# Three DMA latencies in a planner's model, and a new set of ranks, for a chunk-selecting attention with a SwiGLU block behind it

## The chip, the cores and the metric

The kernel runs on one core of a Trainium2 chip. The metric is the device time of one execution in microseconds (us). Beside it stands a profile of one execution; its span is the time from the first to the last instruction.

## The reference

```python
# q, k, v: (4, 8, 768, 64) float32
ub = sum(maximum(q * k_min, q * k_max))     # bound of each query on each chunk of 32 keys
ub = where(causal, ub, -1e9)
top_chunks = argsort(ub)[..., -6:]          # six chunks per query
scores = q @ k.T / 8, kept where the chunk is chosen and key <= query
attn = softmax(scores) @ v                  # -> x: (3072, 512)
xn = x / rms(x) * rms_g
out = (silu(xn @ w_gate) * (xn @ w_val)) @ w_out    # 512 -> 1536 -> 512
```

The inputs are drawn from a normal distribution; the output is float32.

## The kernel before

The 32 heads are handled as 16 pairs of two heads, four pairs to a batch element (`NP`). For each pair the kernel does the following.

- `prep` loads k and q in natural layout (`kload`, `qload`, two DMAs each on SyncE's queue, SP), turns them on TensorE (`kT`, `qT`, L518), copies them from PSUM (`kE`, `qE`, on ScalarE or VectorE), takes the minima and maxima of each chunk (`kmn`, `kmx`), casts k for the scores (`kC`, on GpSimd) and takes the positive part of q (`relu`). `load_v` loads v on GpSimd's queue (POOL).
- The bounds are matmuls (`ub`) of q and its positive part with the minima and the differences. From pair 6 on, two pairs share them (`duo`, L782). They are copied (`ubE`), turned back (`up`), masked (`ubm`), and the sixth largest is found (`max`). `sel` writes 0 or 1 for each chunk beside the cast q (`qN`) in one of two bounce buffers, tile `qn`.
- From pair 3 on, two DMA transposes on SP (`qX`, function `turned`, L558) carry that buffer to the tile `qs`; earlier pairs are turned on TensorE (`selT`, `selC`).
- `scores` multiplies `ke` with `qs` (`sc`, L869), takes the exponential (`exp`, L886), masks the diagonal (`mask`), multiplies with v (`av`, L905), and divides (`xb`).

When all four pairs of a batch element are done, `norm` scales its rows in two halves and turns them: on TensorE for the first batch element (`tp`), by DMA transposes on SP for the others (`xT`, L993). `ffn` then runs 12 steps of `gate` (L1038), `tanh`, `tg`, `val` (L1059), `hh` for each half, and then `po` (L1081), `poE` and the store `out` (L1096). The weights are loaded and cast on POOL's queue in two parts each: `wg`, `wv`, `wo`. 88 matmuls on zeros (`busy`, L346) stand at the lowest rank and fill places where TensorE has nothing else in the plan.

No engine chooses at run time. The function `Order.run` goes through a model of the five engines with a cost for every step, and at each moment takes the ready step with the lowest rank; the order that comes out is emitted once, and each engine works through its own list in that order. A step's rank is the sum of a value for its kind (`RANK`, one table for the first batch element and one for the others) and a value for its place (`TIMES`: `a` is preparation of a pair, `l` its loads, `s` its scores, `n` the norm and `f` the block of a half, `w` the weights). Some copies name two engines and take the one that is free first in the model. A DMA has a load, which the model divides by a rate to get the time on the DMA engines. The four lines that matter here are these:

```python
if s.load > 250000 and dma > t + 3.0:      # a large load waits while the model's DMA is booked
...
if s.load:
    dma = max(dma, t + occ) + s.load / self.RATE      # RATE = 0.21e6 per us
    s.seen = dma + 1.5
```

Of the kernel before, what the change touches and what calls it, by code (L numbers as in the profile page):

```python
# [24 lines left out]

RANK = (
    dict(
        av=322.54, dif=-188.59, eps=-224.95, exp=140.39, kC=-21.2, kE=-26.98, kT=-342.24,
        kload=-68.72, kmn=-914.82, kmx=-233.95, max=-348.3, qC=-27.39, qE=825.6, qN=415.06,
        qT=187.51, qX=464.44, qload=-68.35, relu=-407.91, root=-15.25, sc=372.15, sel=227.85,  # L30
        selC=494.31, selT=-297.7, sq=-125.45, tp=-51.69, tpE=820.25, ub=-638.32, ubE=-943.52,
        ubm=-791.33, up=-275.69, vload=-812.94, xb=-466.6, xs=4.09,
    ),
    dict(
        av=-259.29, dif=-527.49, eps=-1300.51, exp=-91.52, gate=-103.71, hh=53.82, kC=691.52,
        kE=174.13, kT=62.95, kload=344.34, kmn=400.75, kmx=1189.0, mask=146.21, max=-14.89,
        out=-497.46, po=681.38, poE=-473.84, qE=-203.67, qN=402.53, qT=423.51, qX=-950.23,
        qload=228.48, relu=223.42, root=-1267.38, sc=-170.43, sel=672.51, sq=635.32,
        tanh=850.33, tg=69.89, ub=-68.65, ubE=-332.51, ubm=311.82, up=-188.8, val=-96.16,
        vload=-38.35, xT=292.62, xb=-649.94, xs=-92.37,  # L40
    ),
)

TIMES = {
# [15 lines left out]
}  # L60


# [16 lines left out]
class Order:  # L79
# [18 lines left out]
    def run(self, places):  # L98
# [10 lines left out]
        dma = port = 0.0  # L109
# [8 lines left out]
        out = []  # L118
        while len(out) < len(self.steps):
            if not events:  # L120
                stuck = [x for e in waiting for x in waiting[e] if x.start is None]
                raise RuntimeError("no step can go: " + ", ".join(x.name for x in stuck[:20]))
            t = heapq.heappop(events)
            while events and events[0] <= t + 1e-9:
                heapq.heappop(events)
            for e in free:
                if free[e] > t + 1e-9:
                    continue
                best = None
                for s in waiting[e]:  # L130
                    if s.start is not None or s.ready > t + 1e-9:
                        continue
                    if best is not None and (s.rank, s.n) >= (best.rank, best.n):
                        continue
                    if s.load > 250000 and dma > t + 3.0:
                        heapq.heappush(events, dma - 3.0)
                        continue
                    ok, want = True, {}
                    for b in s.opens:
                        if b.slot is not None:  # L140
                            continue
                        if b.sub and count.get(b.sub, 0) + want.get(b.sub, 0) >= self.limits(b.sub, t):
                            ok = False
                        got = sum(h is None or (h.users == 0 and h.done <= t + 1e-9)
                                  for h in held[b.kind])
                        want[b.kind] = want.get(b.kind, 0) + 1
                        if b.sub:
                            want[b.sub] = want.get(b.sub, 0) + 1
                        if got < want[b.kind]:
                            ok = False  # L150
                    if ok:
                        best = s
                if best is None:
                    continue
                s = best
                s.start, s.eng = t, e
                occ = s.occ[e]
                if e == "PE" and t < self.COLD:
                    occ = 2 * occ

                if e == "DVE" and s.port:
                    occ = max(free["POOL"] - t, 0.0) + occ
                    port = t + occ
                elif e == "POOL":
                    occ = max(port - t, 0.0) + occ
                s.seen = t + occ + self.TAIL[e]
                if s.load:
                    dma = max(dma, t + occ) + s.load / self.RATE
                    s.seen = dma + 1.5
                free[e] = t + occ  # L170
                heapq.heappush(events, free[e])
                heapq.heappush(events, s.seen)
                for b in s.opens:
                    if b.slot is None:

                        b.slot = min((i for i, h in enumerate(held[b.kind])
                                      if h is None or (h.users == 0 and h.done <= t + 1e-9)),
                                     key=lambda i: held[b.kind][i].done if held[b.kind][i] else -1.0)
                        held[b.kind][b.slot] = b
                        if b.sub:  # L180
                            count[b.sub] = count.get(b.sub, 0) + 1
                for b in s.bufs:
                    b.users -= 1
                    b.done = max(b.done, s.seen)
                    if b.users == 0 and b.sub:
                        count[b.sub] -= 1
                for x in s.next:
                    x.left -= 1
                    x.ready = max(x.ready, s.seen)
                    if not x.left:  # L190
                        for y in x.engs:
                            waiting[y].append(x)
                        heapq.heappush(events, x.ready)
                for y in s.engs:
                    waiting[y].remove(s)
                out.append(s)
# [5 lines left out]
def kernel(  # L202
# [51 lines left out]
    def add(name, engs, occ, rank, *a, **kw):  # L254
        return order.add(name, engs, occ, rank if isinstance(rank, dict) else {"": rank}, *a, **kw)
# [75 lines left out]
    def make_ident(e):  # L331
# [7 lines left out]
        out=first[:], in_=ident_f[:, 0:1], func=ACT.Exp), [c_id])  # L339
# [80 lines left out]
    def make_tri(e):  # L420
# [11 lines left out]
        load=140000)  # L432
# [37 lines left out]
    def load_v(c, lr):  # L470
        b, h0 = c.b, c.h0

        def go(e):
            nc.gpsimd.dma_start(  # L474
                out=VX[c.v.slot][:, :, 0:D],
                in_=v[b, h0:h0 + 2].rearrange("h (t p) d -> p (h t) d", p=P))

        c.vload = add("v", "POOL", 1.08, rank(lr, b, "vload"), go, c_vx, opens=[c.v], load=450000)

    def prep(c, i0, nb, at, lr):  # L480

# [74 lines left out]
        def turned(bases, buf, dst, name, deps):  # L556
            def move(e, hl):
                nc.sync.dma_start_transpose(  # L558
                    out=dst[c.set.slot][hl][:].rearrange("d (t p) -> d t p", p=P),
                    in_=bases[buf.slot][:, hl * HW:hl * HW + NT * P])  # L560

            return [add(name, "SP", 1.4, rank(at, b, name, hl, "step"), lambda e, hl=hl: move(e, hl),
                        deps, opens=[c.set], uses=[buf], load=200000) for hl in range(2)]

        reds, casts = [], []
        if side_k:
# [589 lines left out]
```

## Time and profile before

| | |
|---|---|
| median of 3 runs | 320.75 us (318.89 to 322.42) |
| the profiled execution | 319.12 us, span 317.4 us, granted clock 1.00 |
| TensorE (PE) | 97% busy, 2835 matmuls |
| VectorE (DVE), ScalarE (ACT), GpSimd (POOL) | 72%, 62%, 32% busy |
| HBM | 28.57 MB read, 6.29 MB written |

In the profile's lines L12 is line 12 of the kernel, `out<-in` are the tiles written and read with their numbers left out, and `<-` behind a wait names what ended it. PE is the queue of matmuls and PEld that of weight loads; SPq and POOLq are queues on which a DMA is issued. A row of the stretches gives the stretch, its length, then the busy time and number of instructions of PE, PEld, DVE, ACT and POOL, the granted TensorE clock, the DMA engines' share and GB/s. A row of the chain or of the timeline gives the start, the duration and the instructions that were merged. A row of groups ends with the total, the mean duration in ns, and the idle time ahead of it.

### The profile page before, as it was taken

The page shows a single profiled execution, that of the slowest core. Times are in us where ns is not written, and L with a number is a line of the kernel's source. Part 1 is how long each engine was busy: PE and PEld are TensorE (multiplying, and loading weights), DVE is VectorE, ACT ScalarE, POOL GpSimd, SP SyncE. Part 2 cuts the span into 40 slices and gives each one's busy share as a digit, 9 for nine tenths or more (in the row PEclk, how much of TensorE's full clock was granted, in tenths as well). Part 3 has the DMA queues.
Part 4 walks back from the last instruction along what each step waited for, and adds up shares of the span by engine and source line. Part 5 has one row for each costly group of instructions (what it writes and reads, how often), then busy time and mean ns, then how long its engine had stood idle before and what let it go on. Part 6 is the DMA issues. An engine that isn't in the chain of part 4 may idle for free.

```text
span 317.4 us, 7652 instructions
## 1 busy us (share of the span) xinstructions
PE 307.9 (97%) x2835; PEld 197.2 (62%) x2856; DVE 227.8 (72%) x650; ACT 197.2 (62%) x429; POOL 102.0 (32%) x157
## 2 busy tenths in 40 slices
PE   8999999999979999999999999999999999999994
PEld 4676778675667656766677555665675565555552
DVE  7799967898779895698995887569657773364410
ACT  5888999784667878863698735863595333233311
POOL 8675532651447544341247401510132000000000
PEclk9999999999999999999999999999999999999999
DMA  9999999999999996992913465200501600101022
GB/s 175 218 188 142 168 170 155 172 154 166 169 154 175 104 132 152 219 207 47 148 31 25 37 174 101 53 33 2 118 16 46 152 5 35 66 0 68 35 98 99
DMA packets 113125, 34.97 MB, mean 110 GB/s; under 512 B 106176, under 2 KB 110016, under 8 KB 113088
## 3 DMA queue, kind: packets, MB, share of 16 engines
q1 hardware_dynamic: 82976, 26.23, 42.9%
q0 software_dynamic: 28512, 7.87, 25.9%
q10 hardware_dynamic: 1600, 0.39, 0.6%
q8 instruction: 22, 0.36, 0.5%
q14 instruction: 15, 0.12, 0.1%
HBM read 28.57 MB, written 6.29 MB: 110 GB/s over the span
## 4 chain that ended last, share of the span: by engine, by line
PE 83%; DMA 6%; ACT 5%; POOL 2%; issue 1%; DVE 1%; ACTq 0%; POOLq 0%
PE po L1081 19%; PE vp L1059 18%; PE gp L1038 18%; PE sc L869 9%; PE av L905 6%; DMA qs<-qn 3%; DMA vx<-in_v_dram 3%; ACT pt L886 3%; PE busy L346 3%; PE ub L782 2%; PE pk L518 2%; PE pq L518 2%; ACT ke L297 1%; POOL ke L301 1%; PE up L804 1%
## 5 line engine op out<-in xcount | busy, mean ns | idle before, releaser
L886 ACT ACTIVATE pt<-sc 128x512 bf16<-128x512 f32 (+3 forms) x192 | 89.3, 580 | 8.4 <-PE sc L869 7.8
L1045 ACT ACTIVATE sg<-gp 128x384 bf16<-128x384 f32 x96 | 47.8, 506 | 55.4 <-PE gp L1038 54.3
L1059 PE MATMUL vp<-xT,wv 128*128 128x384 bf16 x384 | 77.2, 326 | 0.0
L1038 PE MATMUL gp<-xT,wg 128*128 128x384 bf16 x384 | 77.1, 326 | 0.0
L1051 DVE SCALAR_TENSOR_TENSOR tg<-sg,gp 128x384 bf16<-128x384 bf16 x96 | 51.4, 547 | 28.9 <-ACT sg L1045 27.9
L1081 PE MATMUL po<-wo,hh 128*128 128x512 bf16 (+1 forms) x284 | 65.9, 370 | 1.0 <-issue 0.2
L1067 DVE TENSOR_TENSOR hh<-vp,tg 128x384 bf16<-128x384 f32 x96 | 50.9, 549 | 15.2 <-PE po L1081 7.1
L869 PE MATMUL sc<-qs,ke 128*128 128x128 bf16 (+5 forms) x417 | 52.4, 250 | 1.7 <-DMA qs<-qn 1.4
L1038 PEld LDWEIGHTS <-wg 128*128 128x128 bf16 x384 | 35.9, 98 | 24.0 <-issue 1.2
L1059 PEld LDWEIGHTS <-wv 128*128 128x128 bf16 x384 | 36.2, 98 | 22.8
L1081 PEld LDWEIGHTS <-hh 128*128 128x128 bf16 x300 | 29.0, 98 | 28.8 <-issue 1.2
L892 POOL TENSOR_SCALAR_AFFINE_SELECT pt<-pt 128x512 bf16<-128x512 bf16 (+1 forms) x48 | 24.7, 530 | 47.2 <-ACT pt L886 46.9
L905 PEld LDWEIGHTS <-pt 128*128 128x128 bf16 x672 | 32.0, 98 | 10.8 <-POOL pt L892 1.3
L905 PE MATMUL av<-vx,pt 128*128 128x65 bf16 x672 | 37.1, 193 | 1.1 <-DMA vx<-in_v_dram 0.7
L869 PEld LDWEIGHTS <-ke 128*128 128x128 bf16 (+1 forms) x420 | 30.0, 97 | 10.6 <-DMA qs<-qn 1.5
L301 POOL CAST ke<-kt 64x768 bf16<-64x768 f32 x31 | 25.5, 821 | 22.2 <-ACT kt L297 10.6
L299 ACT ACTIVATE osb<-po 128x512 f32<-128x512 f32 (+1 forms) x20 | 11.7, 586 | 30.7 <-PE po L1081 30.6
L346 PE MATMUL busy<-zeros 128*128 128x512 bf16 (+1 forms) x86 | 20.2, 349 | 1.4 <-DVE zeros L341 1.3
L301 POOL CAST qn<-qnat 128x768 bf16<-128x768 f32 x11 | 9.4, 857 | 34.4 <-DMA qs<-qn 34.3
L474 POOL DMA_DIRECT2D vx<-in_v_dram x16 | 16.8, 1049 | 9.3 <-PE av L905 9.0
L982 DVE SCALAR_TENSOR_TENSOR xs<-xb,ri,gains 128x512 bf16<-128x512 bf16 x24 | 17.8, 767 | 1.9 <-DMA xT<-xs 1.6
L926 DVE TENSOR_TENSOR xb<-av,rden 128x384 bf16<-128x384 f32 (+1 forms) x34 | 18.1, 534 | 1.2
(87 smaller groups left out, 306.8 us busy)
## 6 DMA issues: line engine op xcount, KB each, us to landing
out_dram<-osb SPq DMA_DIRECT2D x23, 256.0 KB, 2.1
knat<-in_k_dram SPq DMA_DIRECT2D x30, 192.0 KB, 5.2
qnat<-in_q_dram SPq DMA_DIRECT2D x30, 192.0 KB, 4.9
vx<-in_v_dram POOLq DMA_DIRECT2D x16, 192.0 KB, 6.2
wg<-in_moe_w_gate_dram POOLq DMA_DIRECT2D x2, 768.0 KB, 7.9
wv<-in_moe_w_val_dram POOLq DMA_DIRECT2D x2, 768.0 KB, 7.2
wo<-in_moe_w_out_dram POOLq DMA_DIRECT2D x2, 768.0 KB, 11.9
qs<-qn SPq DMA_TRANSPOSE x26, 2.8
```

Source lines behind the costliest of these rows:

```text
L301: engine[e].tensor_copy(out_, in_)
L346: nc.tensor.matmul(t[:, 0:n], zeros[:, 0:P], zeros[:, 0:n], start=True, stop=True)
L869: nc.tensor.matmul(t[:, x:x + m, :].rearrange("p a b -> p (a b)"), ke[kk, kb * P:(kb + 1) * P], qs[kk, q0 * P:(q0 + m) * P], start=not tri ...
L886: nc.scalar.activation(out=t[:, 0:nn, :], in_=sc.tile[:, 0:nn, :], func=ACT.Exp, scale=SCALE)
L892: nc.gpsimd.affine_select(out=pt.tile[:, 0:nd, :], in_=pt.tile[:, 0:nd, :], compare_op=ALU.is_ge, fill=0.0, base=0, pattern=[[0, nd], [1, ...
L905: nc.tensor.matmul(av.tile[:, qi - i0, :], pt.tile[:, x, :], VX[c.v.slot][:, hl * NT + kb, :], start=(begin and m == 0), stop=(left[0] == ...
L1038: nc.tensor.matmul(t[:], wg[:, g, hs], XT[b].tile[:, g, cols], start=(g == 0), stop=(g == NP - 1))
L1045: nc.scalar.activation(out=t[:], in_=gp.tile[:], func=ACT.Tanh, scale=0.5)
L1051: nc.vector.scalar_tensor_tensor(out=t[:], in0=sg.tile[:], scalar=1.0, in1=gp.tile[:], op0=ALU.add, op1=ALU.mult)
L1059: nc.tensor.matmul(t[:], wv[:, g, hs], XT[b].tile[:, g, cols], start=(g == 0), stop=(g == NP - 1))
L1067: nc.vector.tensor_tensor(out=t[:], in0=vp.tile[:], in1=tg.tile[:], op=ALU.mult)
L1081: nc.tensor.matmul(po.tile[:], hhs[ht].tile[:, th * P:(th + 1) * P], wo[:, ht, c0:c0 + cn], start=(ht == 0), stop=(ht == NHT - 1))
```

## The change

Three numbers of the model change, and both tables of ranks are replaced by others. The steps, their instructions and the functions that emit them stay as they are; which engine makes a copy and where each instruction stands come out of the model again.

```diff
 RANK = (
     dict(
-        av=322.54, dif=-188.59, eps=-224.95, exp=140.39, kC=-21.2, kE=-26.98, kT=-342.24,
...
+        av=490.79, dif=-125.43, eps=-501.19, exp=121.82, kC=-14.0, kE=71.19, kT=-475.34,
...
 TIMES = {
-    "a0": -581.96, "a1": -582.93, "a10": -566.56, "a11": -515.49, "a12": 78.05, "a13": -90.35,
...
+    "a0": 347.98, "a1": 339.24, "a10": 285.13, "a11": 419.78, "a12": 80.87, "a13": 244.6, "a14":
...
                 if s.load:
                     dma = max(dma, t + occ) + s.load / self.RATE
-                    s.seen = dma + 1.5
+                    s.seen = dma + 2.5
...
-        c.vload = add("v", "POOL", 1.08, rank(lr, b, "vload"), go, c_vx, opens=[c.v], load=450000)
+        c.vload = add("v", "POOL", 1.08, rank(lr, b, "vload"), go, c_vx, opens=[c.v], load=600000)
...
             return [add(name, "SP", 1.4, rank(at, b, name, hl, "step"), lambda e, hl=hl: move(e, hl),
-                        deps, opens=[c.set], uses=[buf], load=200000) for hl in range(2)]
+                        deps, opens=[c.set], uses=[buf], load=240000) for hl in range(2)]
```

All entries of `RANK` and `TIMES` have new values; the first line of each stands for them. What this does to the written order, as far as the prediction speaks of it: the first scores stand behind 21.9 us of TensorE work (17.8 before), the scores of pair 5 come after those of pairs 6 and 7, `po` of the first batch element's first half moves from the end of the program to the middle, and the last tile on TensorE is a half `po` tile of the last half.

More of the change, by code (lines that the diff above doesn't have):

```diff
@@ L27 @@
     dict(
-        av=322.54, dif=-188.59, eps=-224.95, exp=140.39, kC=-21.2, kE=-26.98, kT=-342.24,
[L29 to L32, printed above, removed]
+        av=490.79, dif=-125.43, eps=-501.19, exp=121.82, kC=-14.0, kE=71.19, kT=-475.34,
+        kload=87.97, kmn=-874.66, kmx=-133.18, max=-255.93, qC=33.7, qE=845.44, qN=259.26,
+        qT=103.97, qX=345.57, qload=155.84, relu=-499.55, root=257.08, sc=507.34, sel=-26.2,
+        selC=347.24, selT=-149.89, sq=-107.03, tp=-229.09, tpE=761.97, ub=-520.06, ubE=-1040.27,
+        ubm=-713.28, up=-436.98, vload=-613.02, xb=-206.71, xs=77.27,
     ),
     dict(
[L35 to L40, printed above, removed]
+        av=-429.52, dif=-56.01, eps=-1189.67, exp=-151.99, gate=-135.63, hh=1.46, kC=597.83,
+        kE=85.85, kT=171.47, kload=161.93, kmn=616.71, kmx=1102.65, mask=10.34, max=190.89,
+        out=-472.13, po=508.04, poE=-157.3, qE=116.75, qN=127.45, qT=237.68, qX=-949.48,
+        qload=148.26, relu=407.95, root=-1351.08, sc=-302.51, sel=596.25, sq=201.44,
+        tanh=975.67, tg=83.53, ub=-292.03, ubE=-462.41, ubm=235.61, up=30.05, val=-121.8,
+        vload=-3.79, xT=450.72, xb=-572.52, xs=-267.85,
     ),
```

28 rows, old and new, of the table TIMES are left out of this document.

## The prediction

> **What bounds the kernel now.** I read the busy shares first, then PE (TensorE) in five stretches of the span, then the chain that ended last and the waits of PE's two queues, and last the DMAs that these waits name.
>
> ```profile
> span 317.4 us, 7652 instructions
> PE 307.9 (97%) x2835; PEld 197.2 (62%) x2856; DVE 227.8 (72%) x650; ACT 197.2 (62%) x429; POOL 102.0 (32%) x157
> DMA  9999999999999996992913465200501600101022
> PE 83%; DMA 6%; ACT 5%; POOL 2%; issue 1%; DVE 1%; ACTq 0%; POOLq 0%
> ```
> ```profile
> 0.00:32.00 32.00, 29.84 (x306) 19.52 (x308) 27.91 (x92) 24.71 (x50) 23.14 (x42) 1.00 1.28 179
> 32.00:80.00 48.00, 47.62 (x595) 35.00 (x594) 39.93 (x139) 39.02 (x89) 20.42 (x29) 1.00 1.25 166
> 80.00:96.00 16.00, 14.06 (x151) 9.69 (x150) 11.72 (x27) 10.69 (x25) 6.86 (x11) 1.00 1.10 155
> 96.00:312.00 216.00, 214.94 (x1783) 132.34 (x1799) 148.26 (x395) 121.81 (x267) 51.58 (x77) 1.00 0.48 85
> 312.00:317.40 5.40, 1.43 (x9) 0.65 (x7) 0.00 (x0) 0.98 (x2) 0.00 (x0) 1.00 0.20 73
> ```
> The first two columns after the stretch are its length and PE's busy time. PE is busy 307.9 of 317.4 us at a granted clock of 1.00, so 9.5 us are idle: 2.16 before 32 us, 0.38 up to 80, 1.94 between 80 and 96, 1.06 up to 312, and 3.97 in the tail after the last matmul. PE bounds this kernel, and the change gives PE exactly the same instructions in another order. What it can win therefore lies inside those 9.5 us, less a start and a tail that every order has. What it can lose has no such limit. The DMA row says where: the 16 engines are busy at 9 tenths or more for the first 15 slices, about 119 us, and only there does a transfer have to wait for others.
>
> ```profile
> PE sc L869 <- DMA qs<-qn: 1.4, 1, 1.4
> PE busy L346 <- DVE zeros L341: 1.3, 1, 1.3
> PE av L905 <- DMA vx<-in_v_dram: 0.7, 1, 0.7
> 80.82 10.40 DMA qs<-qn
> 72.11 7.87 SPq L498 DMA_DIRECT2D knat<-in_k_dram  x2
> 80.82 6.10 SPq L558 DMA_TRANSPOSE qs<-qn  x2
> 92.08 0.46 DVE L666 SCALAR_TENSOR_TENSOR qn<-m,ubm 128x288 bf16<-128x288 f32 x1 [2.12 <-DMA qs<-qn]
> qs<-qn SPq DMA_TRANSPOSE x26, 2.8
> ```
> The first three rows are all that PE's matmul queue ever waited for that is over 0.3 us. The largest is one event: SP took 7.87 us to issue one k load, the transposes of pair 6 could be issued only behind it, and their landing took 10.40 us where the median is 2.8. PE's wait at the scores was 1.4 us, and VectorE (DVE) stood 2.12 us before it could write the next selection into the same buffer.
>
> **The change part by part.** Only constants change: three latencies in the planner that writes the order, and the ranks it sorts by. I count in "PE work": the rows of PE's own order added up, in which a gate or val group is 0.65 us, four po matmuls 0.86 and the bound of two pairs 1.45.
>
> ```profile
> 72.30 0.65 PE vp L1059 x4
> 72.95 1.45 PE ub L782 x32
> 115.04 5.18 PE po L1081 x24
> ```
> *The longer landings.* A transpose was counted as landing 200000/210000+1.5=2.45 us after its turn on the DMA, and is now counted as 240000/210000+2.5=3.64; a k or q load goes from 3.5 to 4.5, a v load from 3.64 to 5.36.
>
> ```profile
> knat<-in_k_dram SPq DMA_DIRECT2D x30, 192.0 KB, 5.2
> qnat<-in_q_dram SPq DMA_DIRECT2D x30, 192.0 KB, 4.9
> vx<-in_v_dram POOLq DMA_DIRECT2D x16, 192.0 KB, 6.2
> ```
> For the loads (5.2, 4.9 and 6.2 us) the new figures are nearer. For transposes 2.8 lies between old and new. The Trainium skill, DMA: Bandwidth & Descriptors, section "Anatomy of one DMA", gives 2.0 us plus bytes/436e3; for 196608 bytes that is an estimate of 2.45 us, which is the old figure and speaks against counting transposes longer. The trace's 2.8 and 10.40 say that the old figure was too short while the DMA engines are full, so the measurement decides. By the page alone the transposes' part would bring nothing, and the sum below would be 1.0 us higher.
>
> A longer estimate costs no time itself; it spreads the order. After the first loads, a transpose of selections had at least 3.5 us of PE work between issue and first use in the old order and has 4.6 in the new one; k loads at least 5.1 and now 6.5; v loads 6.1 and now 6.9.
>
> *Pair 6.* Old order: q8 and k9 loads stand directly ahead of its transposes on SP. New order: only k9, with 6.2 us of PE work between, and the next load (q11) behind them. Between issue and first use there are 8.8 us of PE work, not 7.9. The wait at 80 to 96 us costs PE 1.94; ends 0 and -1.9. The buffer rotation is as before (pairs 6 and 7 share one bounce buffer) and a 768 KB part of wo starts in the same stretch, so I take half: **-1.0**.
>
> *The weights.* Their place moves the other way. Second half of wg: 19.1 us of PE work between issue and first gate, now 10.3. Second half of wv: 15.9, now 10.2. The last part of wo: 24.8, now 10.5. They go out on GpSimd's (POOL's) queue, behind casts and masks.
>
> ```profile
> wg<-in_moe_w_gate_dram POOLq DMA_DIRECT2D x2, 768.0 KB, 7.9
> DMA to landing us min/median/max: 6.9/7.9/8.9
> DMA to landing us min/median/max: 6.9/7.2/7.5
> DMA to landing us min/median/max: 9.0/11.9/14.8
> ```
> These rows are wg's, then the tiles wg, wv and wo. Against wg's own worst, 8.9, a cover of 10.3 is enough; against wo's worst, 14.8, it is 4.5 short. For the last part of wo the rows are 9.0 (enough) and 14.8 (4.3 short). wg and wv have landed in 6.9 to 8.9 even among loads, and the second wo part that took 9.0 is the one issued in a like place, so I take **0** for both; the ends are +4.5 and +4.3. What hides them is gates, vals and scores of pairs 6 and 7. If wg's part is late, 6 gates and 7 vals queued one behind another on PE wait, and behind them the scores of pair 6; wv's part then has that wait as cover and adds nothing.
>
> *The start.* First loads gain about 1 us of cover, and v of pair 1 moves ahead of q of pair 2. DVE's work up to the selection of pair 2, added in its order, exceeds PE's ahead of the transposes that read it by 3.2 us, and by 2.6 before: **+0.6**. v of pair 0 keeps 6.9 us of cover (7.1 to 7.8 for the first v loads before), so its 0.7 us wait stays: **0**, ends -0.7 and +0.7.
>
> *Who copies.* DVE takes over 3 kt, 5 qt, 5 rt, and one each of ubd, xT and qn, and gives up 4 qs, one dif and two osb.
>
> ```profile
> L301 DVE COPY qt<-pq 128x384 f32<-128x384 f32 x7 | 3.8, 547 | 1.6 <-PE pq L518 1.1 <-PE av L905 0.6
> L636 DVE TENSOR_SCALAR rt<-qt 128x768 f32<-128x768 f32 x3 | 1.7, 557 | 0.3 <-ACT qt L297 0.3
> L301 DVE COPY qs<-st 64x768 bf16<-64x768 bf16 x6 | 3.3, 555 | 0.2
> 152.00:160.00 8.00, 8.00 (x58) 5.50 (x56) 8.00 (x18) 5.20 (x11) 1.48 (x2) 1.00 1.16 164
> 160.00:168.00 8.00, 8.00 (x105) 5.72 (x103) 7.89 (x15) 7.54 (x18) 4.80 (x10) 1.00 0.01 3
> ```
> At some 0.55 us each the sum is +5.2 us on DVE and about as much off ScalarE. DVE is 72% busy, so PE's matmuls hide this: **0**, ends 0 and +5.2, since DVE does have full stretches (8.00 and 7.89 of 8).
>
> *The later stages.* Norm to gate has 14.7 us of PE work at the last batch (12.9 before). The shortest way from the bounds' transposes to the scores is pair 12's, 10.1 us (11.1 before). On it stand four ubm (0.3 each), the maxima (about 2.6), one tg, the selection (0.8) and a landing of 2.8, about 8 us: **0**. The 1.06 us of small gaps stays too; lower end -1.1.
>
> *The end.* Before, the last piece on PE is a full po tile: ScalarE copies it in 0.60 us and its store lands in 2.1. Now it is a half tile.
>
> ```profile
> 312.65 0.38 ACT L299 ACTIVATE osb<-po 128x256 f32<-128x256 f32 x1 [2.88 <-PE po L1081]
> 313.51 0.60 ACT L299 ACTIVATE osb<-po 128x512 f32<-128x512 f32 x1 [0.48 <-PE po L1081]
> out_dram<-osb SPq DMA_DIRECT2D x23, 256.0 KB, 2.1
> out_dram<-osb SPq DMA_DIRECT2D x2, 128.0 KB, 1.8
> ```
> 0.22+0.3: **-0.5**.
>
> Sum: -1.0+0.6-0.5=-0.9 against the profiled execution's 319.12 us (its span of 317.4 and 1.7 around it), 318.2. That execution lies 1.63 below the median of 320.75; on the median's footing I forecast **319.9 us**, no change that can be told.
>
> **The rivals.**
> *A, slower: a weight part lands late.* Place: the first gate on the second half of wg, and the first po. It decides from a landing of 10.3 us, and 10.5 for wo. If the slowest part's 14.8 holds at one place, +4.4 and 324.3; at both, +8.8 and 328.7. For it: full DMA engines, and in the new order five k and q loads stand in the 10 us ahead of wg's part. Against: 6.9 to 8.9 in the same company. By the page named above, 1.57 MB read would take an estimated 5.6 us and A could not occur; the trace's 9.0 to 14.8 disagree.
> *B, slower: DVE becomes the bound.* If all its 5.2 us fall where DVE is full, 319.9+5.2=325.1. For it: the two full windows. Against: added up in order, DVE's work leads PE's by no more by 105 us of PE work than before.
> *C, faster: every wait goes.* -1.9 at pair 6, -0.7 at v, -1.1 of small gaps, -0.5 at the end, nothing at the start: -4.2 and 316.5. For it: covers that are longer nearly everywhere. Against: it must all come together, and every order makes waits of its own.
> *D, the change does nothing:* PE's work is the same and undisturbed transposes land in 2.8 whatever is assumed; 320.3 with the shorter end.
>
> **How the numbers follow.** About 1% (3.2 us) is what a measurement of this kernel tells from no change. The forecast has 0.36, with a range of its own of 318 to 323, and D 0.09: within 1% together 0.45. C has 0.17, because a gain of over 3.2 needs three quarters of all that can be won. A has 0.19 and B 0.19: slower 0.38. The range reaches from C's time, 316.5, to 328.0, just short of both places of A; some 0.05 lie below and 0.12 above.
>
> **What would show it.** PE busy stays near 308 us at clock 1.00. The wait of the scores on qs shrinks below 1.4 us and DVE's 2.12 us goes; if not, that step is wrong. wg's second part lands within 10 us, and no gate or po waits on a DMA; a PE wait on wg, wv or wo of 2 us or more is A. DVE near 233 us with PE waiting on DVE in the middle would be B. The tail is 3.5 us, not 3.97. A PE idle time of over 13 us makes the forecast wrong, wherever it stands.

## The result and the profile after

The changed kernel takes 318.70 us (median of 20 runs, 318.08 to 319.69) and the kernel before, on the same chip, 321.82 us (20 runs, 318.27 to 326.56). The ratio is 0.9934, 95% interval 0.9912 to 0.9955: 0.66% faster, inside the 1% that was called no change. The ratio is taken over the runs within 1.5% of the fastest of their kernel, which leaves out the slowest of the kernel before, and so it lies nearer to 1 than the 0.990 of the medians. The profiled execution takes 318.09 us against 319.12 before, so only 1.0 of the 3.1 us between the medians can be seen between the two profiles; the rest is that the changed kernel's runs lie within 1.6 us of each other and those of the kernel before within 8.3.

The page of the changed kernel, then its stretches (columns as for the kernel before):

```profile
span 316.4 us, 7669 instructions
PE 310.2 (98%) x2856; PEld 197.4 (62%) x2856; DVE 235.6 (74%) x659; ACT 194.5 (61%) x420; POOL 102.1 (32%) x157
DMA  9999999999969999999940036540040046000202
PE 91%; ACT 4%; DVE 4%; issue 0%; ACTq 0%; DVEq 0%
```
```profile
0.00:32.00 32.00, 29.99 (x284) 18.02 (x285) 26.41 (x96) 23.14 (x45) 19.77 (x38) 1.00 1.20 179
32.00:80.00 48.00, 47.31 (x598) 35.17 (x595) 42.75 (x122) 38.55 (x87) 24.01 (x32) 1.00 1.02 165
80.00:96.00 16.00, 16.00 (x133) 10.41 (x132) 12.93 (x33) 8.46 (x19) 4.37 (x7) 1.00 1.20 128
96.00:312.00 216.00, 216.00 (x1845) 133.27 (x1842) 153.52 (x412) 123.62 (x270) 53.91 (x82) 1.00 0.50 87
312.00:316.40 4.40, 0.87 (x8) 0.53 (x6) 0.00 (x0) 0.77 (x2) 0.00 (x0) 1.00 0.30 103
```
TensorE (PE) is idle for 2.01, 0.69, 0, 0 and 3.53 us. The idle stretch between 80 and 96 us (1.94 before) is gone, and DMA is no longer in the chain (6% before). The 1.06 us of small gaps up to 312 us are gone too, but they were hardly idle time: 2856 of 2856 matmuls are recorded here and 2835 before, and nearly all of these gaps (about 0.05 us each) stand within a few rows of a place where a record is missing. For the same reason PE's busy time seems to rise from 307.9 to 310.2.

PE's waits in the changed kernel, all of them over 0.1 us:

```profile
PE busy L346 <- DVE zeros L341: 1.3, 1, 1.3
PE st L695 <- DVE selq L680: 0.7, 1, 0.7
PE gp L1038 <- ACT xT L297: 0.3, 1, 0.3
PE av L905 <- ACT pt L886: 0.2, 1, 0.2
```
None of them is on a DMA. Next the issues on SP's queue around pair 6's transposes, and the landings (minimum, median, maximum) of the tiles wg, wv, wo and qs:

```profile
81.41 2.59 SPq L558 DMA_TRANSPOSE qs<-qn  x2
84.09 1.62 SPq L498 DMA_DIRECT2D qnat<-in_q_dram  x2
```
```profile
DMA to landing us min/median/max: 6.8/7.7/8.6
DMA to landing us min/median/max: 6.8/7.8/8.8
DMA to landing us min/median/max: 7.4/7.6/7.7
DMA to landing us min/median/max: 2.5/2.9/5.5
```
The longest landing of a transpose is 5.5 us where it was 10.40, and wo's parts land in 7.4 to 7.7 where they took 9.0 to 14.8. The DMA row is as full as before (9 tenths or more in 19 of the first 20 slices), so it is not that the engines have room.

The chain's rows that tell where the order stands, and the tail:

```profile
71.89 1.45 PE ub L782 x32
109.01 1.08 PE ub L782 x17
```
```profile
311.83 1.04 PE L1081 MATMUL po<-wo,hh 128*128 128x256 bf16 x8
312.52 0.82 ACT L299 ACTIVATE osb<-po 128x256 f32<-128x256 f32 x2 [1.59 <-PE po L1081]
```
I compare the start of a row with the PE work that the order has ahead of it (counted as in the prediction). Before: 72.95 us with 66.2 ahead, 115.04 with 105.4, so PE runs 6.75 and then 9.6 us late. After: 71.89 with 63.3, 109.01 with 100.2, so 8.6 and then 8.8 late. The start became 1.85 us worse; the stretch from 72 to 110 us became 2.65 better; from there to the last matmul some 0.25 worse; the tail 0.44 better. Together -1.0, which is what the spans show. Little of the loss at the start is idle time (2.01+0.69 us up to 80 us, 2.16+0.38 before); the rest is spread over PE rows that take longer than counted.

### The profile page after: what moved, and what is told of

Read it like the earlier page. It is cut to its first block, busy times and chain, and to the rows that moved or that the text cites. A ratio compares the mean times of both kernels' runs of the same rounds, so it can differ in the third digit from the quotient of the medians.

```text
span 316.4 us, 7669 instructions
## 1 busy us (share of the span) xinstructions
PE 310.2 (98%) x2856; PEld 197.4 (62%) x2856; DVE 235.6 (74%) x659; ACT 194.5 (61%) x420; POOL 102.1 (32%) x157
## 3 DMA queue, kind: packets, MB, share of 16 engines
q0 software_dynamic: 28512, 7.87, 26.0%
## 4 chain that ended last, share of the span: by engine, by line
PE 91%; ACT 4%; DVE 4%; issue 0%; ACTq 0%; DVEq 0%
PE gp L1038 20%; PE vp L1059 20%; PE po L1081 20%; PE sc L869 12%; PE av L905 7%; PE pk L518 3%; PE pq L518 3%; PE busy L346 2%; PE ub L782 2%; PE up L804 1%; ACT ke L297 1%; PE ub L724 1%; DVE ku L549 1%; DVE kmx L547 1%; ACT pt L886 1%; PE sc L875 1%
## 5 line engine op out<-in xcount | busy, mean ns | idle before, releaser
L886 ACT ACTIVATE pt<-sc 128x512 bf16<-128x512 f32 (+2 forms) x192 | 88.9, 594 | 10.3 <-PE sc L869 9.6
L1051 DVE SCALAR_TENSOR_TENSOR tg<-sg,gp 128x384 bf16<-128x384 bf16 x96 | 52.3, 550 | 33.1 <-ACT sg L1045 31.4
L1038 PE MATMUL gp<-xT,wg 128*128 128x384 bf16 x384 | 74.9, 326 | 0.3 <-ACT xT L297 0.3
L1059 PE MATMUL vp<-xT,wv 128*128 128x384 bf16 x384 | 74.8, 326 | 0.0
L1067 DVE TENSOR_TENSOR hh<-vp,tg 128x384 bf16<-128x384 f32 x96 | 51.9, 553 | 10.5 <-PE vp L1059 8.3
L869 PE MATMUL sc<-qs,ke 89*128 89x128 bf16 (+4 forms) x420 | 53.6, 251 | 0.0
L869 PEld LDWEIGHTS <-ke 89*128 89x128 bf16 (+1 forms) x420 | 29.4, 97 | 7.3 <-issue 1.0
L299 ACT ACTIVATE osb<-po 128x512 f32<-128x512 f32 (+1 forms) x22 | 12.8, 582 | 30.8 <-PE po L1081 29.4
L346 PE MATMUL busy<-zeros 128*128 128x512 bf16 (+1 forms) x88 | 19.2, 349 | 1.3 <-DVE zeros L341 1.3
L549 DVE TENSOR_REDUCE ku<-kt 128x24 f32<-128x768 f32 (+1 forms) x17 | 15.2, 897 | 2.7 <-ACT kt L297 2.6
```

What stands on the lines that cost most here:

```text
L346: nc.tensor.matmul(t[:, 0:n], zeros[:, 0:P], zeros[:, 0:n], start=True, stop=True)
L869: nc.tensor.matmul(t[:, x:x + m, :].rearrange("p a b -> p (a b)"), ke[kk, kb * P:(kb + 1) * P], qs[kk, q0 * P:(q0 + m) * P], start=not tri ...
L886: nc.scalar.activation(out=t[:, 0:nn, :], in_=sc.tile[:, 0:nn, :], func=ACT.Exp, scale=SCALE)
L1038: nc.tensor.matmul(t[:], wg[:, g, hs], XT[b].tile[:, g, cols], start=(g == 0), stop=(g == NP - 1))
L1051: nc.vector.scalar_tensor_tensor(out=t[:], in0=sg.tile[:], scalar=1.0, in1=gp.tile[:], op0=ALU.add, op1=ALU.mult)
L1059: nc.tensor.matmul(t[:], wv[:, g, hs], XT[b].tile[:, g, cols], start=(g == 0), stop=(g == NP - 1))
```

## The experiments

Two theories stood at first for pair 6: SP's loads ahead of the transposes made them late, as the prediction had it, or it was the 768 KB weight part that is in flight beside them. The experiments move single steps of the finished order; `done` is the list that `Order.run` returns, and `spot` finds the n-th step of a name at a place.

**e3: before, the first wo part later.**

```diff
     done = order.run(PLACE)
+    s = done.pop(spot("wo", "w3"))
+    done.insert(spot("qX", "a6", 1) + 1, s)
```


> The kernel before, with one weight DMA (the first wo part) issued behind the transposes of pair 6 instead of ahead of them, some 10 us of PE work later; it still has 27 us of PE work before its first use. Theory (the gain of the change is mainly the late transposes of pair 6, and these were late because the DMA engines were full): they land in under 6 us instead of 10.4, PE's idle time between 80 and 96 us falls from 1.94 to under 0.5, the profile comes to about 317, and the runs scatter less than before's 318 to 326. Rival 1 (they were late because SP itself stood 7.87 us at the k load ahead of them): that issue stays above 5 us and PE's wait stays above 1.2. Rival 2 (the gain sits in the tail and the start): no change of the median, about 321.5.

Measured: 323.96 us (12 runs, one of them an outlier of 1142.53), ratio 1.0053 (1.0010 to 1.0096). From SP's timeline, the chain, PE's waits, wo's landings and the stretches after the wait:

```profile
74.05 1.42 SPq L498 DMA_DIRECT2D knat<-in_k_dram  x2
81.82 2.54 SPq L558 DMA_TRANSPOSE qs<-qn  x2
```
```profile
83.08 11.58 DMA qs<-qn
```
```profile
PE av L905 <- POOL pt L892: 3.9, 1, 3.9
```
```profile
DMA to landing us min/median/max: 10.1/11.7/13.3
```
```profile
96.00:98.00 2.00, 1.45 (x22) 1.46 (x23) 1.97 (x6) 0.49 (x2) 0.86 (x2) 0.65 0.78 162
98.00:100.00 2.00, 1.78 (x16) 1.27 (x15) 1.14 (x4) 1.69 (x4) 1.31 (x3) 0.50 0.57 125
```
Neither side had it. The k load ahead, which had held SP for 7.87 us, is issued in 1.42, and SP is free at 75.47 us. Still the transposes go out no earlier (81.82 us, 80.82 in the kernel before), and the second of them takes 11.58 us to land (the first 3.58): now both wo parts, issued at 82.43 and 83.65, are in flight beside it. So SP's slow load was not the cause. The wait is longer than before because GpSimd (POOL) stands at its cast into `qn` until the transposes have landed, and the masks of the exponentials are queued behind it. And the wait costs twice: the granted clock falls to 0.50 behind it.

**e4: after, two loads ahead of pair 6's transposes.** The q and k loads of pair 11 go in front of them.

```diff
+    for name in ("qload", "kload"):
+        s = done.pop(spot(name, "l11"))
+        done.insert(spot("qX", "a6"), s)
```


> The changed kernel, with the q and k loads of pair 11 issued directly ahead of pair 6's transposes on SP instead of behind them. Theory: the transposes are issued and land later, more than 6 us instead of at most 5.5, PE waits 1 to 3 us for them at the scores of pair 6 where it did not wait at all, the median rises from 318.7 to 320 or 321.5, and the runs scatter over more than 2 us. Rival (loads ahead of the transposes do not matter as long as the weights are not in flight): 318.7, PE waits under 0.3 us.

Measured: 318.94 us, ratio 0.9908 (0.9876 to 0.9940). The longest landing of a transpose is 7.0 us (5.5 in the changed kernel) and PE waits for no DMA. But the loads stand ahead in the list only: SP issues them at 66.35 and 71.70 us and is free at 74.89, 7 us before the transposes go out at 81.94. So loads that are issued in good time do no harm that shows; a load that holds SP until the transposes are due was not tried here, and what speaks against that cause is e3.

**e8: before, the second wo part later**, clear of pair 6.

```diff
+    s = done.pop(spot("wo", "w2"))
+    done.insert(spot("v", "l9") + 1, s)
```


> The kernel before, with one weight DMA (the second wo part issued) moved from just behind the issue of pair 6's transposes to behind the v load of pair 9, some 16 us later; nothing else differs. Theory (a weight part in flight beside a pair's transposes makes these land 10 us late and more, which holds up the scores, GpSimd's next cast and the masks behind it): the transposes of pair 6 land in under 6 us, PE's idle time between 80 and 96 us falls below 0.6, the granted clock is 0.998 or more in most runs, and the median falls from 322.0 to 318.5 to 320. Rival 1 (the gain of the change came from its other order as a whole): the median stays above 321. Rival 2 (the wait only moves to the transposes of pairs 8 and 9 or to the first po, which the part now meets): PE idles 1.5 us or more after 105 us.

Measured: 321.36 us (316.67 to 323.92), ratio 0.9952 (0.9897 to 1.0006), which leaves it open whether this gains; 318.5 to 320 was expected. Its two fastest runs, 316.67 and 317.13, lie below every run of the changed kernel. The profiled execution, 322.19 us, is one of its longer ones. Pair 6's transposes now land in 4.7 us on the mean, but those of pair 5 met the second wv part and the first wo part. From the chain, PE's waits and wo's landings:

```profile
68.38 15.43 DMA qs<-qn
```
```profile
PE sc L869 <- DMA qs<-qn: 3.0, 2, 2.5
```
```profile
DMA to landing us min/median/max: 11.3/13.7/16.0
```
Where the weight part went out of the way the landing is short. The longest landing of all runs is not the work of the edit: up to the moved part, at about 81 us, this run has the order of the kernel before, and there the same two transposes of pair 5, beside the same two parts, landed in 7.6 and 10.3 us where they took 13.6 and 15.4 here. One order can thus land up to 6 us later in one execution than in another.

**e11: before, both wo parts clear** of pairs 5 and 6.

```diff
+    s = done.pop(spot("wo", "w2"))
+    done.insert(spot("v", "l9") + 1, s)
+    s = done.pop(spot("wo", "w3"))
+    done.insert(spot("kC", "a9", 1) + 1, s)
```


> The kernel before with both wo parts moved: the first to behind the casts of pair 9 (about 88 us, after pair 6's transposes have landed), the second to behind the v load of pair 9 (about 98 us). The transposes of pairs 5 and 6 then meet no wo part. Theory (weight parts in flight beside the transposes were what the kernel before lost, in its time and in its scatter): both land in 8 us or less, PE idles under 1 us between 56 and 112 us, the granted clock is 0.997 or more in most runs, and the median is 317 to 319.5, below before's 321.7 and perhaps below the changed kernel's 318.7. Rival (the parts only find other victims, pair 7's transposes or the first po): PE waits 1.5 us or more at these places, and the median stays above 320.5.

Measured: 325.62 us, ratio 1.0109 (1.0072 to 1.0146). The stretches, SP's timeline and PE's waits:

```profile
56.00:80.00 24.00, 23.90 (x259) 15.85 (x258) 21.28 (x78) 16.60 (x38) 10.19 (x16) 1.00 1.13 152
80.00:96.00 16.00, 16.00 (x184) 11.59 (x183) 13.49 (x31) 12.19 (x28) 8.70 (x13) 1.00 0.91 119
96.00:112.00 16.00, 8.43 (x71) 5.25 (x77) 5.69 (x11) 6.29 (x13) 5.36 (x8) 0.69 1.25 165
```
```profile
93.22 14.27 SPq L498 DMA_DIRECT2D qnat<-in_q_dram  x6
```
```profile
PE pq L518 <- issue: 7.6, 1, 7.6
```
PE is busy 39.90 of the 40 us from 56 to 96 (37.96 in the kernel before): the cause is confirmed in the old order. But the total came out much as the rival had it: the moved part met three q loads at 93 us, SP needed 14.27 us to issue them, and PE waited 7.6 us at the turning of q (the trace calls it issue), with a granted clock of 0.69 in that stretch. A weight part has to pass somewhere, and the new order has it pass where it meets nothing that is needed soon.

**e9: after, the second wo part put in the way** of pair 6's transposes.

```diff
+    s = done.pop(spot("wo", "w2"))
+    done.insert(spot("v", "l5") + 1, s)
```


> The changed kernel, with its second wo part issued ahead of the landing of pair 6's transposes (behind the v load of pair 5, some 19 us earlier) instead of after pair 7's. Theory: the transposes of pair 6 land in 9 us or more instead of at most 5.5, GpSimd's cast for pair 7 waits as long, PE waits 1 us or more at the scores or at the products behind the masks, the granted clock falls below 0.997 in some runs, and the median rises from 318.7 to 320 or 323. Rival (the longer covers of the new order absorb it): under 319.3, and PE waits under 0.5 us.

Measured: 319.78 us, ratio 0.9956 (0.9926 to 0.9986). The landings of qs and the stretch:

```profile
DMA to landing us min/median/max: 2.5/3.0/9.0
```
```profile
80.00:96.00 16.00, 15.34 (x123) 9.66 (x122) 12.90 (x34) 7.83 (x17) 3.22 (x5) 1.00 1.27 166
```
The slow landing comes back (9.0 us, before 10.40) and with it 0.66 us of idle time, a third of what the old order lost there. VectorE stands 1.1 us before it can write the next selection, and PE 0.5 at a gate that waits for VectorE's product `hh` behind it. Direction and place are as expected, the price is smaller than the 1 us or more that was expected; by the intervals of the times alone it could not be told from the changed kernel.

**e5 and e10: after, the second wv part late**, to try rival A's mechanism: once behind `dif` of pair 8, once behind the first wo part.

```diff
+    s = done.pop(spot("wv", "w1"))
+    done.insert(spot("dif", "a8") + 1, s)     # e5
+    done.insert(spot("wo", "w3") + 1, s)      # e10
```


> The changed kernel, with the second part of wv issued some 5 us later on GpSimd's queue (behind the differences of pair 8). Theory (a weight part lands 6.8 to 8.8 us after its issue, and PE has no slack behind it): PE waits 2 to 4 us at the first val that uses it, and the total rises by as much, to 320.7 to 322.7. Rival (PE's wait is made up later, because ScalarE and VectorE set the pace there): the wait shows but the median stays within 0.5 us of 318.7.

> The changed kernel, with the second part of wv issued behind the first-issued wo part, so that PE waits longer for it than the 1.80 us that it waited when the part was issued behind the differences of pair 8. Theory (a long enough wait of PE costs twice: the wait itself, and about 4 us at a granted clock of 0.5 behind it): PE waits 3 to 7 us in one piece, the granted clock falls to 0.5 for some 4 us after it, and the median rises by the wait and 1 to 2 us more, to 323 to 328. Rival (the clock falls only where several short waits follow each other, as in the run with fewer fillers): the clock stays at 0.998 or more, and the median rises by the wait alone.

Measured: e5 320.28 us, ratio 0.9950 (0.9923 to 0.9978); e10 327.94 us, ratio 1.0215 (1.0169 to 1.0262). PE's waits of e5, then of e10, then the stretches of e10 around its wait:

```profile
PE vp L1059 <- DMA wv<-in_moe_w_val_dram: 1.8, 1, 1.8
```
```profile
PE vp L1059 <- DMA wv<-in_moe_w_val_dram: 6.5, 1, 6.5
```
```profile
84.00:86.00 2.00, 0.00 (x0) 0.00 (x0) 0.00 (x0) 0.00 (x0) 0.00 (x0) 1.00 1.15 176
86.00:88.00 2.00, 0.04 (x1) 0.04 (x2) 0.00 (x0) 0.00 (x0) 0.00 (x0) 0.70 1.39 154
88.00:90.00 2.00, 2.00 (x7) 0.99 (x8) 0.54 (x2) 0.00 (x0) 0.00 (x0) 0.50 1.67 151
90.00:92.00 2.00, 2.00 (x8) 0.92 (x7) 1.04 (x3) 0.00 (x0) 0.24 (x1) 0.50 1.63 160
92.00:94.00 2.00, 2.00 (x9) 0.96 (x8) 1.58 (x3) 0.00 (x0) 0.59 (x1) 0.59 1.44 170
```
In e5 1.8 us of wait cost 1.6 us at a clock of 1.00, somewhat less than the 2 to 4 that were expected. In e10 6.5 us of wait cost 9.2: the clock stays at half for some 6.8 us behind the beginning of the dip (0.70, 0.50, 0.50, 0.59 in four stretches of 2 us). Rival A's mechanism is real and would have been expensive; it did not occur because the weight parts of the changed kernel land in 8.8 us at most.

**e6: after, with the copies on the engines of before.** The steps kE, qE, relu, ubE, tpE, poE and selC keep the new order, and each goes to the engine that it has in the kernel before (some 5 us, net, from VectorE back to ScalarE).

```diff
     done = order.run(PLACE)
+    for e, ns in (("ACT", [...]), ("DVE", [...])):
+        for n in ns:
+            order.steps[n].eng = e
```


> The changed kernel in its order, but each PSUM copy (kt, qt, rt, ubs, ubd, xT, qs, osb) on the engine that the kernel before used for it: some 5 us of work go back from VectorE to ScalarE. Theory (VectorE's extra work is hidden): within 0.7 us of 318.7, either way. Rival (VectorE's load costs time in the changed kernel): 0.7 us or more below, 318.0 or less.

Measured: 324.49 us, ratio 1.0111 (1.0069 to 1.0154), 5.8 us over the changed kernel. The stretch from 32 to 48 us and the first gate, of the changed kernel and then of e6, and a wait of e6:

```profile
32.00:48.00 16.00, 15.90 (x258) 12.92 (x255) 12.35 (x41) 15.50 (x37) 8.82 (x11) 1.00 1.06 139
```
```profile
61.00 0.81 PE L1038 MATMUL gp<-xT,wg 128*128 128x384 bf16 x4 [0.32 <-ACT xT L297]
```
```profile
32.00:48.00 16.00, 15.14 (x232) 11.68 (x232) 8.69 (x34) 15.88 (x38) 8.43 (x10) 1.00 1.03 138
```
```profile
64.86 0.81 PE L1038 MATMUL gp<-xT,wg 128*128 128x384 bf16 x4
```
```profile
PE av L905 <- ACT pt L886: 2.6, 7, 0.6
```
Neither side had it. With the old engines ScalarE is busy 15.88 of 16 us, PE waits 2.6 us for its exponentials where it waited 0.2, and the first gate comes 3.9 us later. The copies are not hidden in this order: on which engine they stand is part of it.

**e13 and e14: after, 1.4 us more off ScalarE.** Two qt and one ubs copy between 34 and 47 us go to VectorE; in e14 12 of the 19 matmuls on zeros at 52 us (1.3 us) are left out as well.

```diff
+    for n in (412, 473, 541):
+        order.steps[n].eng = "DVE"
...
     for s in done:
+        if 306 <= s.n <= 317:      # e14 only
+            continue
```


> The changed kernel with three copies between 34 and 47 us (two qt, one ubs, together 1.4 us of ScalarE) moved to VectorE, TensorE's order untouched. Theory: ScalarE bounds the stretch from 28 to 50 us (15.50 us busy of 16 between 32 and 48), but TensorE has matmuls on zeros there that fill what it would wait, so moving copies alone brings at most 0.5 us: 318.3 to 318.9, and TensorE's idle time between 32 and 80 us falls below 0.69. Rival: VectorE (12.35 of 16 there) is the tighter one, and its norm of the first batch element comes later: over 319.5.

> The same three copies on VectorE, and 12 of the 88 matmuls on zeros (1.3 us) left out of the run of 19 that stands at 52 us. Theory: ScalarE's 1.4 us are what those 12 covered, so TensorE gains about 1 us: 317.4 to 318.2, clock 1.00. Rival: what stands behind the matmuls on zeros is VectorE's norm and not ScalarE's exponentials, so the same wait for the norm opens (over 0.8 us) and the time is 318.5 to 320.

Measured: e13 318.91 us, ratio 0.9951 (0.9916 to 0.9985); e14 318.70 us, ratio 0.9914 (0.9882 to 0.9945): no gain over 318.70. PE's waits of e14:

```profile
PE tp L1004 <- DVE xs L982: 0.7, 2, 0.5
PE busy L346 <- DVE xb L926: 0.7, 1, 0.7
```
The 1.3 us that were left out come back as 1.4 us of waits for VectorE's division and norm of the first batch element. So with the old engines for all copies PE waits for ScalarE (e6), while relieving ScalarE between 34 and 47 us does not help: in e14 it is VectorE's chain that ends next.

**e7: after without those 19 matmuls on zeros.**

```diff
     for s in done:
+        if 306 <= s.n <= 324:
+            continue
```


> The changed kernel without the 19 matmuls on zeros that stand in one row (52.3 to 54.4 us of the profile) ahead of the first scores of pair 4; they feed nothing. Theory (the scores were ready, and 2.07 us of filling delayed them and all behind them): the scores start up to 2 us earlier and the total falls by 1 to 2 us, to 316.7 to 317.7, at a granted clock of 1.00. Rival 1 (something else is not ready then, such as the transposes of pair 4 or the norm's rows): PE stands idle for those 2 us instead, 318.7. Rival 2 (the idle time costs clock): the granted clock falls below 0.99 and the time rises.

Measured: 319.83 us, ratio 0.9931 (0.9904 to 0.9959), 1.1 over the changed kernel. PE's longest new wait, and the stretches:

```profile
PE tp L1004 <- DVE xs L982: 1.4, 2, 1.2
```
```profile
54.00:56.00 2.00, 0.81 (x8) 0.35 (x7) 2.00 (x5) 2.00 (x7) 0.87 (x2) 0.96 1.12 186
56.00:58.00 2.00, 1.77 (x18) 1.51 (x17) 2.00 (x4) 1.63 (x5) 2.00 (x3) 0.50 1.20 242
58.00:60.00 2.00, 2.00 (x26) 1.70 (x25) 0.61 (x2) 1.09 (x3) 1.14 (x3) 0.69 0.65 142
```
2.1 us of matmuls that compute nothing were taken out, and the kernel got slower: the gap opens as a wait, and the clock is at half for some 3.4 us (2 us at 0.50 and part of the next 2).

**e12: the changed kernel again** in another session.

> The changed kernel again, unedited, beside the run above on the same chip. Every theory: 318.1 to 319.7, median near 318.7, granted clock 0.998 or more.

Measured: 318.89 us, ratio 0.9942 (0.9907 to 0.9976). Eleven of the 12 runs take 318.70 to 319.87 us; one takes 322.39, at a mean granted clock of 0.994, so the changed kernel is not free of such runs.

## Why the prediction held, and where its steps failed

*The total.* On the profiled execution's footing the sum was 318.2 us, and it is 318.09. So close a hit is luck: the gain at pair 6 was put 1.65 us too small and the loss ahead of the first bound of two pairs 1.25 too small, and the two errors nearly cancel. On the median's footing the forecast was 319.9 and the median is 318.70. The step between the two failed: the 1.63 us by which the profiled execution stood under the median was carried over, and the changed kernel's profiled execution stands only 0.61 under its own.

Why the changed kernel's runs agree so well is shown in part. All of its 20 runs have a mean granted clock of 0.998 or more (in e12 11 of 12). Of the 27 runs of the kernel before that e3's ratio rests on, 16 have less and a median of 322.02 us, against 320.88 for the other 11. That waits of PE bring such a dip is seen in e3, e7, e10 and e11. That the dips in the old order's runs come from landings like the 10.40 us one, longer in some runs than in others, fits e8, whose trace is that of the old order up to 81 us; a run of the unchanged kernel with a dip was not traced.

*The longer landings, pair 6 (-1.0; ends 0 and -1.9).* The event and the place were right: the wait on qs is gone and DVE's 2.12 us with it. The term was under-sized, since taking half was a choice and all of it came, and the stretch from 72 to 110 us gained about 2.65 against the old order. The reason given, SP's loads directly ahead, was wrong: e3 refutes it, and e8, e9 and e11 show the weight parts beside the transposes. The prediction named the wo part in that stretch, but as a reason against the gain; it was the lever. The new order issues its first wo part at 75 us, has it landed before 83 us, 1.4 us after pair 6's transposes go out, and issues the second at 97 us. The formula that the prediction took from the Trainium skill, DMA: Bandwidth & Descriptors, section "Anatomy of one DMA", is stated there for DMAs that GpSimd issues, and the transposes are issued by SP; for them 2.45 us is an estimate by analogy. The fastest landings here, 2.5 us, come near it; the 10.40 is far off.

*The weights (0; ends +4.5 and +4.3).* Right. wg's and wv's second parts landed in 8.6 and 6.8 us, under the covers of 10.3 and 10.2, and the last part of wo in 7.4. e5 and e10 show that a late part costs what rival A said, and more where the clock falls.

*The start (+0.6).* The size came out at the place that it counted, and a second place was left out. Before, the first gate stands at 55.37 us with 49.3 of PE work ahead, 6.1 late; after, the first scores of pair 4 stand at 54.24 with 47.5 ahead, 6.7 late, which is the +0.6. But the first gate, now behind these scores, stands at 61.00 with 52.6 ahead, 8.4 late, and 1.2 us of these further 1.7 remain at the first bound of two pairs. From 54.73 us on ScalarE is busy without a break with the exponentials and then with the copies ahead of that gate:

```profile
54.73 5.34 ACT L886 ACTIVATE pt<-sc 128x512 bf16<-128x512 f32 x12 [0.42 <-PE sc L869]
```
The count set only VectorE's work against PE's, and ended before this place. That relieving ScalarE between 55 and 61 us would win the 1.2 us was not tried. The 0.6 is in part luck as well: PE waits 0.7 us for VectorE's selection (the row `st` above), which is the kind of wait that was counted, but the v wait that was to stay is gone (-0.7), and up to 32 us PE's weight loads wait 1.1 us for ScalarE's exponentials instead.

*Who copies (0; ends 0 and +5.2).* No cost of it shows, but the reasoning was wrong. It counted the move as something that PE hides and that can only cost. e6 shows that, without it, the new order costs 5.8 us more. VectorE's busy time is 235.6 us where 233 was forecast, and PE waits on it, behind the first 1.3 us, for 0.7: rival B did not occur.

*The later stages (0).* Nearly right: 0.25 us were lost. The 1.06 us of gaps were hardly there to win, so rival C's -4.2 counted a thing that does not exist.

*The end (-0.5).* 3.53 us instead of 3.97: -0.44.

*Rival D*, that the change does nothing, is out: DMA's 6% of the chain is gone.

Ranks and latencies could not be told apart. With any one of the three latencies set back, the new ranks give no complete order, nor do the old ranks with a new latency; so whether the longer latencies, or other ranks that happened to be found with them, took the weight parts out of the way stays open. None of the versions that were run has a lower median than the changed kernel.

## What to carry to other kernels

Where the DMA engines are full, look for a transfer's delay in the bulk transfer that is in flight beside it, and do not stop at what stands ahead of it on its own queue; moving the bulk helps only if the place it goes to has nothing urgent. A long wait of TensorE can have a second price in the clock behind it, and a wait that hangs on a landing can differ from run to run, so one profile may not show what an order costs: read the granted clock and the spread of the runs beside the trace. Engine choices of small copies belong to an order, and their worth is measured in that order and in both directions.

## What the runs showed of the hardware

A DMA transpose of 2.8 us (median) took 8.3 and 10.40 us in the kernel before beside wo parts, 3.58 and 11.58 in e3 beside two, and 13.6 and 15.43 in e8 beside a wv and a wo part, where the same order had given 7.6 and 10.3. So the number of parts alone does not set the time. With no weight part in flight the longest landing in the kernel before was 7.4 us, among the first loads (issued at 29.90 us). SP needed 7.87 us (8.96 in e8) to issue one pair's k load while the first wo part was in flight, and 1.42 and 1.43 in e3 and e11, where that part was moved; in e11 six issues of q loads took 14.27 us.

The clock fell to 0.50 after idle time of very different length: in e7 after 1.63 us of it in pieces (0.44 between 52 and 54 us and 1.19 up to 56), in e3 after 3.9, in e10 after 6.5; but not in e5 after 1.80 us in one piece. Reckoned from the rows, it stayed at half for about 3.4 us in e3 and e7 and for 6.8 in e10. The Trainium skill, TensorE: Matmul & The Clock Gate, section "What's actually happening", has the clock at half after an idle window of about 3.4 us and at full after a busy one of the same length, the windows running freely. The half, the 3.4 and twice 3.4 us agree; that a window has to be idle as a whole does not agree with e7. Where the bound lies was not measured.
